# Attention, router and experts on one core: the first expert's first two columns made together between the turns, a tighter account for the search, and a last scatter of half rows

## The chip, the cores and the metric

One core of one Trainium2 chip runs the whole program. The metric is the time of one execution on the device in microseconds (us); lower is better. Times of a run vary: three runs of the kernel before took 895.05, 895.93 and 897.81 us.

## The reference

Two stages, cut to what matters. Attention over 8 x 12 heads of 448 tokens and 64 dimensions, with RMS norms on q and k, gives x of 3584 tokens by 768. A mixture of experts then assigns each token to one of 8 experts, greedily from the largest logit down, at most 448 tokens per expert, and sends it through that expert alone:

```python
logits = x @ w_gate
order = np.argsort(-logits.flatten())
for idx in order:
    tok, e = idx // E, idx % E
    if assigned[tok] >= 0 or counts[e] >= cap:
        continue
    assigned[tok] = e; counts[e] += 1
for e in range(E):
    h = np.maximum(x[assigned == e] @ w1[e], 0.0)
    out[assigned == e] = h @ w2[e]
```

## The kernel before, in words

The first 400 us are the attention, which the change does not touch. It leaves in DRAM `xd`, a row per token with two float16 halves (high and low part) of its 768 values, and the logits in SBUF.

**Router.** The greedy assignment is done expert by expert: the expert that is full first is found, its 448 tokens are listed, they and the expert are taken out, and the search starts again. `Router.phase(k)` (L1508) makes the steps of the k-th search. The first (k = 0) runs by itself between attention and experts. Searches 1 to 7 run as *hops* beside the experts' matmuls. A search of k = 1 to 6 has `open_bests` (VectorE finds each token's best open expert), then eight digits of four bits; each digit is `count` (four short TensorE matmuls, L1471, then VectorE's `own` and `cs`), `total` (one matmul, L1485, then VectorE's `ged`, L1488) and `accumulate` (one matmul, L1492, then VectorE's `v` and the comparison `cmp`, L1455). After the last digit come `place`, `slots`, the listing, `lists` (L1643) and `joined` (L1657), which leaves `idx`, 448 token numbers as 128 partitions by 4 columns; the fourth column uses 64 partitions.

**Experts.** Class `Experts`, L1700 on. The weights of the k-th expert come in eight pieces of 768 KB (`fetch`, L1736, issued by SyncE into four `stage` buffers; pieces 0 to 3 are w1, two columns each, 4 to 7 are w2). `split` (L1753) has ScalarE write the high float16 part and VectorE, in two halves, the low part (L1766). The second half's end frees the buffer for the piece four later. `gather` (L1772) brings the expert's rows by four indirect DMAs of GpSimd, chunks of 128, 128, 128 and 64 tokens. They have to be turned: by a transposing DMA, or, for experts 0 and 1, by TensorE (`turn_here`, L1788): per chunk twelve transposes into two PSUM tiles, one of the high half (i = 0) and one of the low (i = 1), each then copied into `xt` by ScalarE (L1801) or VectorE (L1803).

`hidden(k, f)` (L1817) makes column f of eight: 128 hidden values for all 448 tokens, 18 matmuls (L1848: six blocks, high by high, high by low, low by high), then ScalarE's relu into `hh` and VectorE's rest `hl`. For the first column of the first expert it has four parts of 128, 128, 128 and 64 tokens, with the turns of chunks 1, 2 and 3 between them; chunk 0 is turned ahead of it, in `run`. `result(k, c)` (L1851) makes 128 tokens' output in two halves of 384 columns (L1865), or for the last 64 tokens both halves at once on two halves of the array (L1874), copies them out scaled, and scatters the rows by an indirect DMA of GpSimd (L1884). In the last expert's last rows ScalarE copies one half and VectorE the other (L1880).

**The order of the work.** Every engine executes its instructions in the order in which the program issues them, so where the program puts a hop decides who waits. An account does this. `tick` (L1892) adds the estimated length of each matmul to a time `t`. Three lists hang on it: `fills` (a piece's `split`, at a given `t`), `lows` (VectorE's subtractions and the next fetch, not before an estimated time `low[0]`, 4 us later while the search has hops left, since `WAIT` = 4.0), and the `queue` of hops. A hop goes when `t >= due`. Ahead of a hop with TensorE work the oldest ready entry of `lows` is issued (L1904 on):

```python
if pe:
    for low in [low for low in self.lows if low[0] <= self.t + pe][:1]:
        self.low(low)
f()
self.t += pe
if dve:
    self.free = max(self.free + pre, self.t + self.REACH) + dve
    self.due = self.free + self.SLACK[len(self.router.e) > 1]
```

`free` is the account's guess of when VectorE is through, `SLACK` (L1917) what is added before TensorE may ask for the result: 0.3 us in search 1 and 0.45 us later. The copies of `turn_here` are not in `free`.

**Between router and first expert**, in `run` (L1980 on): the first search, the first two fetches, warm matmuls of 512 columns whose result nobody reads (`warm`, numbers in `WARM`), the gather, two more fetches that wait for the third chunk of rows, `open_bests` with the first comparison of search 1, four warm matmuls, `split` of piece 0, its two subtractions with the first `count` between them, three warm matmuls, the turn of chunk 0, the first `total`, and `t` is set to 0. From there the loop over experts runs, with `fills` for pieces 1 to 7 at 4.2 i - 2.3.

## Time and profile before

| | before |
|---|---|
| median of three runs (lowest, highest) | 895.93 us (895.05, 897.81) |
| the profiled execution: its time | 895.94 us |
| its span, first to last instruction | 894.0 us |
| mean granted TensorE clock (share of full speed) | 0.986 |
| TensorE busy | 857.7 us, 96% of the span |
| VectorE, ScalarE, GpSimd busy | 639.5, 470.1 and 384.4 us |
| first turns of the first expert | at 424.36 us |
| last matmul begins | at 884.86 us |

A row of a timeline has the start in us from the span's start, the length in us, the engine (PE is TensorE, PEld its weight load, DVE VectorE, ACT ScalarE, POOL GpSimd, SP SyncE; a q behind it is the engine's queue of instructions), the line of the kernel, the operation, what it writes and reads, and how many instructions are merged in the row. In square brackets stands the idle time before it and what ended that. Ends of matmuls are modelled: in a stream, the distance from start to start is what one costs. A row of a stage by windows has the stretch, its length, and for each engine the busy time and the number of instructions, then the granted clock (1.00 is 2.4 GHz, 0.50 is 1.2 GHz), the share of the DMA engines and GB/s.

### The profile page before, as it was taken

What the parts mean: (1) busy time and instruction counts of PE and PEld (TensorE: products, weight loads), DVE (VectorE), ACT (ScalarE), POOL (GpSimd) and SP (SyncE); (2) the same over time, 40 slices, a digit from 0 to 9 for tenths busy, and PEclk for the clock granted to TensorE, in tenths of its full rate; (3) what the DMA queues carried; (4) which work ended last, traced back from release to release, by engine and by line L of the source; (5) the groups of instructions that cost most, each with busy time, mean ns of one, the idle gap of its engine ahead of it and who ended that gap; (6) DMA issues with size and microseconds to landing.
All of it is one profiled execution on the core that took longest, in us unless ns stands there. A gap on an engine that the chain in (4) does not pass through costs nothing.

```text
span 894.0 us, 27400 instructions
## 1 busy us (share of the span) xinstructions
PE 857.7 (96%) x11671; PEld 554.2 (62%) x11673; DVE 639.5 (72%) x1573; ACT 470.1 (53%) x752; POOL 384.4 (43%) x390
## 2 busy tenths in 40 slices
PE   6999999999999999986999999999999999999996
PEld 2567676777777777874656565565555655555553
DVE  8999999989988986658877776776768567253100
ACT  6987887888778777550534333332434323343110
POOL 8899998889889887001012030110211021200001
PEclk9999999999999999996999999999999999999999
DMA  7679998999999987424647095693928659690001
GB/s 190 165 169 202 185 198 176 205 192 208 194 208 214 171 190 176 76 95 137 237 140 259 10 290 179 203 256 106 295 78 261 181 174 271 215 239 39 27 18 45
DMA packets 253011, 153.61 MB, mean 172 GB/s; under 512 B 178650, under 2 KB 240090, under 8 KB 251866
## 3 DMA queue, kind: packets, MB, share of 16 engines
q1 hardware_dynamic: 247832, 129.62, 60.4%
q0 software_dynamic: 4640, 22.02, 7.5%
q8 instruction: 91, 1.49, 0.7%
q14 instruction: 30, 0.25, 0.1%
q10 hardware_dynamic: 418, 0.23, 0.1%
HBM read 94.42 MB, written 22.02 MB: 130 GB/s over the span
## 4 chain that ended last, share of the span: by engine, by line
PE 56%; issue 22%; DVE 8%; DMA 4%; POOL 4%; ACT 3%; SPq 2%; POOLq 0%; ACTq 0%; DVEq 0%
PE ph L1848 13%; PE po L609 12%; PE psc L574 11%; PE py L1865 11%; DVE mx L555 3%; PE py L1874 2%; PE pm L544 2%; DMA q<-qs 2%; POOL out_dram L1884 2%; POOL rows L1781 1%; ACT e L585 1%; PE psc L544 1%; DMA q<-mt 1%; DMA stage<-in_moe_w_dram 1%; SPq L255 1%
## 5 line engine op out<-in xcount | busy, mean ns | idle before, releaser
L1848 PE MATMUL ph<-xt,w1h 128*128 128x448 f16 (+2 forms) x804 | 210.0, 344 | 0.1
L609 PEld LDWEIGHTS po<-v,e 128*64 128x64 f32 (+1 forms) x5376 | 172.2, 137 | 40.0 <-issue 20.4
L609 PE MATMUL po<-v,e 128*64 128x65 f32 (+1 forms) x5376 | 185.9, 223 | 1.6 <-DVE xt L376 1.0
L585 ACT ACTIVATE e<-psc 128x896 f32<-128x896 f32 x168 | 151.1, 915 | 47.1 <-PE psc L574 41.0
L574 PE MATMUL psc<-q,k 128*64 128x448 f16 x1344 | 155.9, 354 | 2.5 <-issue 1.3
L1884 POOL DMA_INDIRECT out_dram<-y,idx x32 | 33.4, 1042 | 285.3 <-ACT y L1867 250.3
L1848 PE MATMUL ph<-xt,w1l 128*128 128x448 f16 (+2 forms) x402 | 135.0, 344 | 0.0
L1865 PE MATMUL py<-w2h,hh 128*128 128x384 f16 x384 | 125.0, 326 | 0.0
L1865 PE MATMUL py<-w2l,hh 128*128 128x384 f16 x384 | 125.0, 326 | 0.0
L1865 PE MATMUL py<-w2h,hl 128*128 128x384 f16 x384 | 125.0, 326 | 0.0
L1848 PEld LDWEIGHTS <-w1h 128*128 128x128 f16 x804 | 73.9, 97 | 62.3 <-issue 1.9
L555 DVE TENSOR_REDUCE mx<-pm 128x2 f32<-128x896 f32 x96 | 104.0, 1084 | 10.6 <-PE pm L544 8.0
L1836 ACT ACTIVATE hh<-ph 128x448 f16<-128x448 f32 x64 | 34.8, 543 | 140.7 <-PE ph L1848 131.3
L1865 PEld LDWEIGHTS <-hh 128*128 128x128 f16 x768 | 73.5, 97 | 46.6
L574 PEld LDWEIGHTS <-k 128*64 128x64 f16 x1344 | 74.3, 110 | 32.4 <-issue 7.3
L1867 ACT ACTIVATE y<-py 128x384 f32<-128x384 f32 x48 | 23.5, 490 | 126.2 <-PE py L1865 100.4
L1781 POOL DMA_INDIRECT rows<-xd,idx x32 | 31.7, 991 | 125.8 <-DMA stage<-in_moe_w_dram 40.8
L555 DVE TENSOR_REDUCE mx<-psc 128x2 f32<-128x896 f32 (+1 forms) x74 | 77.8, 1056 | 3.2 <-PE psc L544 2.6
L1766 DVE SCALAR_TENSOR_TENSOR w2l<-stage,w2h 128x768 f16<-128x768 f32 x64 | 60.2, 952 | 24.3 <-ACT w2h L1762 24.3
L1838 DVE SCALAR_TENSOR_TENSOR hl<-ph,hh 128x448 f16<-128x448 f32 x64 | 39.4, 619 | 49.8 <-ACT hh L1836 49.6
L1766 DVE SCALAR_TENSOR_TENSOR w1l<-stage,w1h 128x768 f16<-128x768 f32 x64 | 59.3, 951 | 3.7 <-ACT w1h L1762 3.7
L1848 PEld LDWEIGHTS <-w1l 128*128 128x128 f16 x402 | 38.2, 97 | 30.9 <-issue 0.5
(300 smaller groups left out, 1438.9 us busy)
## 6 DMA issues: line engine op xcount, KB each, us to landing
stage<-in_moe_w_dram SPq DMA_DIRECT2D x64, 768.0 KB
vraw<-in_v_dram SPq DMA_DIRECT2D x24, 384.0 KB
xd<-xb SPq DMA_DIRECT2D x8, 1152.0 KB
qkraw<-in_q_dram SPq DMA_DIRECT2D x23, 384.0 KB
qkraw<-in_k_dram SPq DMA_DIRECT2D x23, 384.0 KB
vraw<-in_v_dram SPq DMA_DIRECT2D x24, 64.0 KB
xd<-xm SPq DMA_DIRECT2D x16, 96.0 KB
qkraw<-in_k_dram SPq DMA_DIRECT2D x22, 64.0 KB
```

The costliest lines, as they stand in the source:

```text
L544: nc.tensor.matmul(p[:, i, :448], qt[:, 128 * u:128 * u + 128], kt[:, 448 * s:448 * s + 448], start=True, stop=True)
L555: self.nc.vector.tensor_reduce(m, p[:, :k, :448], axis=AX.X, op=OP.max)
L574: nc.tensor.matmul(p[64 * h:64 * h + 64, i, :448], kt[:, a, n + 64 * h:n + 64 * h + 64], qt[:, a, 448 * s:448 * s + 448], start=st, stop=n ...
L585: self.nc.scalar.activation(e, p[:, :, :448], AF.Exp, scale=scale)
L609: self.nc.tensor.matmul(self.po(pair)[64 * n:64 * n + 64, w], self.T["e", d][r, i, q:q + 64], self.v1[g % 2][r, self.slot(a, u, s)], start ...
L1766: self.later(0.93, lambda w=w: self.nc.vector.scalar_tensor_tensor(l[:, w], v[:, w], self.WS, h[:, w], op0=OP.mult, op1=OP.subtract), k, i)
L1781: nc.gpsimd.indirect_dma_start(out=g[:n, c, :], out_offset=None, in_=self.xd, in_offset=bass.IndirectOffsetOnAxis(ap=idx[:n, c:c + 1], axi ...
L1836: nc.scalar.activation(hh, whole, AF.Relu)
L1838: self.later(0.6, lambda: nc.vector.scalar_tensor_tensor(hl, whole, 0.0, hh, op0=OP.max, op1=OP.subtract), k, 3.5, f)
L1848: nc.tensor.matmul(p, a[:, i, c], x[:, b, o], start=j == 0, stop=j == 17)
L1865: nc.tensor.matmul(p, a[:, f, s], b[:, f, o], start=st, stop=sp)
L1884: st = nc.gpsimd.indirect_dma_start(out=self.out, out_offset=bass.IndirectOffsetOnAxis(ap=self.router.idx[k][:n, c:c + 1], axis=0), in_=y[ ...
```

## The change

Four things are done.

- The start (`columns`, new, called at the first expert's begin). Columns 0 and 1 are made in three strips of 128, 128 and 192 tokens, in the order: turns of chunks 0 and 1, strip 0 of columns 0 and 1, turn 2, strip 1 of column 0, turn 3, strip 1 of column 1, strip 2 of both. For k = 0, ScalarE copies each chunk's high half and VectorE its low half. Within a strip the six matmuls with `w1l` come last. Pieces 0 and 1 are both split by ScalarE ahead of it, and piece 0's subtractions are issued there; piece 1's and the next two fetches go into `lows` for 2.5. `t` is 0 ahead of the first turn, and the first hop falls due at 2.5 (`SECOND`).
- `open_bests` of search 1 is a hop of its own, issued by hand; the first digit with its comparison is the next, left to the account. One warm matmul of four and the later three are gone.
- `SLACK` goes from 0.3 and 0.45 to 0.1 and 0.15.
- The last 64 tokens of the last expert: ScalarE copies both halves in one instruction, 128 partitions of 384 columns, and the scatter writes 128 half rows, with a list of half rows (`halves`) that search 7 makes out of `idx` with a few VectorE instructions (`both`, `half`, `halves`).

```diff
--- before.py
+++ after.py
@@ -1651,6 +1651,8 @@
                 f()
             both = st["both"] = self.small("both", [128, 2, 8, 2], BF)
             V.tensor_copy(both.rearrange("p i a t -> p (i a t)"), p)
+            if last:
+                V.tensor_copy(both[:, :, 7], q[:, :, 6])
             if k == 0:
                 st["gone"]()
 
@@ -1672,6 +1674,12 @@
             V.tensor_copy(lo, q[:, 1])
             idx = self.idx[k] = self.w.tile([128, 4], I32, name="idx", bufs=8)
             V.tensor_tensor(idx, q[:, 0], lo, op=OP.add)
+            if last:
+                half = self.small("half", [128, 1])
+                V.memset(half, 0.0)
+                V.memset(half[64:], 1.0)
+                self.halves = self.small("halves", [128, 1], I32)
+                V.scalar_tensor_tensor(self.halves, idx[:, 3:4], 2.0, half, op0=OP.mult, op1=OP.add)
 
         def many(*fs):
             return lambda: [f() for f in fs]
@@ -1689,7 +1697,11 @@
         else:
             begin, count, total, accumulate = self.digit_search(st)
             n = len(self.DIGITS)
-            hops.append((many(self.open_bests, lambda: self.digit(0), begin), 0.0, best + 1.0, 0.0))
+            if k == 1:
+                hops.append((self.open_bests, 0.0, best, 0.0))
+                hops.append((many(lambda: self.digit(0), begin), 0.0, 1.0, 0.0))
+            else:
+                hops.append((many(self.open_bests, lambda: self.digit(0), begin), 0.0, best + 1.0, 0.0))
             for i in range(n):
                 hops.append((lambda i=i: count(i), 0.12, counted, 0.0 if i else 1.05))
                 hops.append((lambda i=i: total(i), 0.12, 0.25, 0.0))
@@ -1797,12 +1809,12 @@
                                     idn[:n, :n])
             self.t += 0.34
             o = self.T["xt", k][:, 6 * i:6 * i + 6, 128 * c:128 * c + n]
-            if i and (k or c < 2) or k + c == 0:
+            if bool(i) == (k > 0):
                 nc.scalar.activation(o, p, AF.Copy)
             else:
                 nc.vector.tensor_copy(o, p)
 
-    WARM = 6, 4, 5, 4, 3
+    WARM = 6, 4, 5, 3
 
     def warm(self, n, after=None):
 
@@ -1819,34 +1831,41 @@
         if f == 0:
             T["hh", k] = self.w.tile([128, 8, 448], F16, name="hh", bufs=1)
             T["hl", k] = self.w.tile([128, 8, 448], F16, name="hl", bufs=1)
-        x = T["xt", k]
-        whole = self.ps.tile([128, 512], F32, name="ph", bufs=3)[:, :448]
-        c = slice(128 * f, 128 * f + 128)
-        parts = 4 if k + f == 0 else 1
         if k and f == 0 and k not in self.early:
             for n in self.HERE.get(k, ()):
                 self.turn_here(k, n)
-        for q in range(parts):
-            o = slice(448 * q, 448) if parts == 1 else slice(128 * q, min(448, 128 * q + 128))
-            if parts > 1:
-                for n in ((1,), (), (2, 3), ())[q]:
-                    self.turn_here(k, n)
-            self.column(k, whole[:, o], x, c, o, parts)
+        whole = self.begun.pop(f) if k == 0 and f in self.begun else self.column(k, f)
         hh, hl = T["hh", k][:, f], T["hl", k][:, f]
         nc.scalar.activation(hh, whole, AF.Relu)
         self.scalar(0.55)
         self.later(0.6, lambda: nc.vector.scalar_tensor_tensor(hl, whole, 0.0, hh, op0=OP.max, op1=OP.subtract), k, 3.5, f)
 
-    def column(self, k, p, x, c, o, parts):
+    def column(self, k, f, o=slice(0, 448), p=None):
+
         nc, T = self.nc, self.T
-        h, l = T["w1h", k], T["w1l", k]
-        each = [((h, i, i), (h, i, 6 + i), (l, i, i)) for i in range(6)]
-        order = [w for e in each for w in e]
-        if parts > 1:
-            order = [w for e in each for w in e[:2]] + [e[2] for e in each]
+        h, l, x = T["w1h", k], T["w1l", k], T["xt", k]
+        if p is None:
+            p = self.ps.tile([128, 512], F32, name="ph", bufs=3)[:, :448]
+        c, n = slice(128 * f, 128 * f + 128), o.stop - o.start
+        order = [w for i in range(6) for w in ((h, i, i), (h, i, 6 + i), (l, i, i))]
+        if n < 448:
+            order.sort(key=lambda w: w[0] is l)
         for j, (a, i, b) in enumerate(order):
-            nc.tensor.matmul(p, a[:, i, c], x[:, b, o], start=j == 0, stop=j == 17)
-            self.tick(0.189 if parts == 1 else 0.05)
+            nc.tensor.matmul(p[:, o], a[:, i, c], x[:, b, o], start=j + o.start == 0, stop=j == 17 and o.stop == 448)
+            self.tick(0.189 if n == 448 else max(0.057, n / 2400 + 0.003))
+        return p
+
+    SECOND = 2.5
+
+    def columns(self):
+
+        q = slice(0, 128), slice(128, 256), slice(256, 448)
+        for what in (0, 1, (0, 0), (1, 0), 2, (0, 1), 3, (1, 1), (0, 2), (1, 2)):
+            if isinstance(what, int):
+                self.turn_here(0, what)
+            else:
+                f, n = what
+                self.begun[f] = self.column(0, f, q[n], self.begun.get(f))
 
     def result(self, k, c):
         nc, T = self.nc, self.T
@@ -1874,16 +1893,18 @@
                         nc.tensor.matmul(p[64 * half:64 * half + 64], a[:, f, s],
                                          b[:, f, 384 * half:384 * half + 384], start=st, stop=sp)
                     self.tick(0.183)
-            for half in range(2):
-                o, i = y[:64, 384 * half:384 * half + 384], p[64 * half:64 * half + 64]
-                if k == 7 and half:
-                    nc.vector.tensor_scalar(o, i, sc, None, op0=OP.mult)
-                else:
+            if k == 7:
+                nc.scalar.activation(y[:, :384], p, AF.Copy, scale=sc)
+            else:
+                for half in range(2):
+                    o, i = y[:64, 384 * half:384 * half + 384], p[64 * half:64 * half + 64]
                     nc.scalar.activation(o, i, AF.Copy, scale=sc)
         nc.gpsimd.memset(self.spacer, 0.0)
-        st = nc.gpsimd.indirect_dma_start(
-            out=self.out, out_offset=bass.IndirectOffsetOnAxis(ap=self.router.idx[k][:n, c:c + 1], axis=0),
-            in_=y[:n], in_offset=None)
+        if k == 7 and n < 128:
+            to, at, y = self.out.rearrange("n (h d) -> (n h) d", h=2), self.router.halves, y[:, :384]
+        else:
+            to, at, y = self.out, self.router.idx[k][:n, c:c + 1], y[:n]
+        st = nc.gpsimd.indirect_dma_start(out=to, out_offset=bass.IndirectOffsetOnAxis(ap=at, axis=0), in_=y, in_offset=None)
         for o in self.scat:
             self.tc.declare_no_dep(st.ins, o.ins, reason="every token is in one list once")
         self.scat.append(st)
@@ -1914,7 +1935,7 @@
             self.due = self.free + self.SLACK[len(self.router.e) > 1]
 
 
-    REACH, SLACK, WAIT = 0.25, (0.3, 0.45), 4.0
+    REACH, SLACK, WAIT = 0.25, (0.1, 0.15), 4.0
 
     def scalar(self, us):
 
@@ -1980,7 +2001,7 @@
     def run(self):
         self.t = self.due = self.free = self.act = 0.0
         self.lows = []
-        self.now, self.waiting, self.early = 0, [], set()
+        self.now, self.waiting, self.early, self.begun = 0, [], set(), {}
         first, slots, rest = self.router.phase(0)
         first()
         self.load(0)
@@ -1998,16 +2019,14 @@
         hops = phases[0][0]
         hops.pop(0)[0]()
         self.warm(self.WARM[3], self.router.score[:, 0, 0:8])
-        self.step(0, 0)
-        first, second = self.lows[:2]
-        self.low(first)
-        hops.pop(0)[0]()
-        self.low(second)
-        self.warm(self.WARM[4])
-        self.turn_here(0, 0)
-        hops.pop(0)[0]()
-        self.t = self.due = self.free = 0.0
-        for i in range(1, 8):
+        for i in range(2):
+            self.step(0, i)
+        for low in self.lows[:2]:
+            self.low(low)
+        self.lows = [(self.SECOND, *low[1:]) for low in self.lows]
+        self.t = self.free = self.act = 0.0
+        self.due = self.SECOND
+        for i in range(2, 8):
             self.fill(self.FIRST * i - 2.3, 0, i)
         for k in range(1, 8):
             hops, ends, listing, lists, joined = phases[k - 1]
@@ -2022,6 +2041,8 @@
         for k in range(8):
             self.now = k
             self.start()
+            if k == 0:
+                self.columns()
             for f in range(8):
                 self.need(k, f // 2)
                 for low in [low for low in self.lows if low[3][1:] == (3.5, f - 2)]:
```

## Rows read from the trace of the kernel before

**Rows 1.** Page, costliest groups: line, engine, out<-in, count | busy us, mean ns | idle before.

```profile
L1848 PE MATMUL ph<-xt,w1h 128*128 128x448 f16 (+2 forms) x804 | 210.0, 344 | 0.1
```

**Rows 2.** Timeline of PE, from the first turns to the third column.

```profile
424.36 0.83 PE L1796 MATMUL py<-ident,rows 128*128 128x128 f16 x12
...
425.60 0.17 PE L1485 MATMUL rp<-cs,sums 128*128 128x8 f16 x1 [0.41 <-DVE cs L1481]
...
426.77 0.77 PE L1848 MATMUL ph<-xt,w1h 128*128 128x128 f16 x11
...
428.73 1.48 PE L1796 MATMUL py<-ident,rows 128*128 128x128 f16 x24
...
432.23 0.17 PE L1485 MATMUL rp<-cs,sums 128*128 128x8 f16 x1 [0.37 <-DVE cs L1481]
...
432.37 0.54 PE L1848 MATMUL ph<-xt,w1h 128*128 128x448 f16 x2
...
435.94 0.54 PE L1848 MATMUL ph<-xt,w1h 128*128 128x448 f16 x2
```

**Rows 3.** Timeline of ACT, the first split and the first turn's copies.

```profile
420.34 1.48 ACT L1762 ACTIVATE w1h<-stage 128x1536 f16<-128x1536 f32 x1 [4.20 <-DMA stage<-in_moe_w_dram]
425.21 1.51 ACT L1801 ACTIVATE xt<-py 128x768 f16<-128x768 f16 x2 [3.38 <-PE py L1796]
```

**Rows 4.** Timeline of PEld, the weight loads of the second turn.

```profile
425.60 0.68 PEld L1796 LDWEIGHTS <-rows 128*128 128x128 f16 x12 [0.53 <-DMA rows<-xd,idx]
```

**Rows 5.** Timeline of DVE in the same stretch.

```profile
424.38 0.67 DVE L1289 TENSOR_SCALAR digi<-keyi 128x28 int32<-128x28 int32 x7
...
429.26 1.55 DVE L1803 COPY xt<-py 128x768 f16<-128x768 f16 x4 [1.72 <-PE py L1796]
430.73 0.95 DVE L1766 SCALAR_TENSOR_TENSOR w1l<-stage,w1h 128x768 f16<-128x768 f32 x1
```

**Rows 6.** PE by timeline and by windows, where the granted clock fell and rose.

```profile
391.61 0.84 PE L720 MATMUL psc<-ident,xb 128*128 128x128 f16 x12
...
398.00:398.50 0.50, 0.50 (x32) 0.50 (x26) 0.00 (x0) 0.00 (x0) 0.00 (x0) 0.72 1.08 428
...
415.84 1.91 PE L1814 MATMUL py<-rows,ones 128*128 128x512 bf16 x4 [0.22 <-issue]
...
418.00:419.00 1.00, 0.70 (x19) 0.62 (x20) 0.74 (x6) 0.00 (x0) 0.00 (x0) 0.65 1.07 357
...
421.91 1.02 PE L1814 MATMUL py<-rows,ones 128*128 128x512 bf16 x4
```

**Rows 7.** Timelines of DVE and PE, a comparison and its count in a later search.

```profile
592.19 0.39 DVE L1455 TENSOR_TENSOR cmp<-v,rows 128x448 bf16<-128x448 bf16 x1
...
593.00 0.27 PE L1471 MATMUL rp<-oh,cmp 128*128 128x64 bf16 x4
```

**Rows 8.** Timeline of PE behind the second expert's turns.

```profile
485.41 0.33 PE L1874 MATMUL py<-w2l,hh 128*64 128x384 f16 x2
485.89 0.17 PE L1485 MATMUL rp<-cs,sums 128*128 128x8 f16 x1
```

**Rows 9.** Timelines of ACT, DVE, POOL at the end; landing of L1884; the end's drains.

```profile
881.21 0.49 ACT L1867 ACTIVATE y<-py 128x384 f32<-128x384 f32 x1 [3.36 <-PE py L1865]
885.28 0.48 ACT L1882 ACTIVATE y<-py 64x384 f32<-64x384 f32 x1 [3.58 <-PE py L1874]
...
885.80 0.56 DVE L1880 TENSOR_SCALAR y<-py 64x384 f32<-64x384 f32 x1 [26.79 <-ACT y L1882]
...
881.97 0.97 POOL L1884 DMA_INDIRECT out_dram<-y,idx  x1 [6.74 <-ACT y L1867]
...
886.63 0.90 POOL L1884 DMA_INDIRECT out_dram<-y,idx  x1 [3.60 <-DVE y L1880]
...
DMA to landing us min/median/max: 3.0/3.7/5.9
...
L2080 POOLq DRAIN  x1: 6525/6525/6525, 886.4 to 886.4; - x1
```

## The prediction, before the change was run

> **What bounds the kernel now.** I read the list of costliest groups first. It names TensorE: the largest group, 804 of the experts' matmuls, has 0.1 us of idle time ahead of all of them together [rows 1], so from the first expert's second column on, work saved on another engine is worth nothing, and only three things can move the time: when that full stretch begins, waits that the change puts into it, and what follows its last matmul. I then read TensorE's timeline around the beginning. The first expert's turns begin at 424.36, its second column at 432.37 and its third at 435.94 [rows 2]. A 128-column matmul takes (0.77 - 0.22) / 10 = 0.055 us there, so a strip of 18 takes 1.0; the second column, 18 matmuls of 448 columns, takes 3.57 with three search steps in it, 0.19 each; two chunks' turns take 1.48, 0.7 a chunk [rows 2]. A strip of 192 columns lies between: 0.055 + (0.19 - 0.055) x 64 / 320 = 0.082, 1.5 a strip. Work of TensorE from 424.36 to 435.94 is four turns (2.8), the first column (3.5) and the second (3.4), with seven steps some 10.0 of 11.6 us. The rest is waiting: 0.41 and 0.37 us for `cs` of the search [rows 2], some 0.5 us at 426.3 while ScalarE copies both halves of the first chunk, 0.75 us each [rows 3].
>
> **The change, the start.** Going are the three last warm matmuls, the first digit's begin, count and total ahead of and between the turns, and the two-copies-on-one-engine order. Coming is a written order: turns 0 and 1, strips (column 0, chunk 0) and (1, 0), turn 2, (0, 1), turn 3, (1, 1), then both 192-wide strips. TensorE's work is the same: two columns of 1.0 + 1.0 + 1.5 = 3.5 against 3.5 + 3.4. What can be won is waiting.
>
> Turn 0 may go some tenths earlier without the warm matmuls, but that is worth nothing, since turn 1 loads its weights only at 425.60, after 0.53 us put down to the gathered rows [rows 4]. From there: turn 1 to 426.3; two strips to 428.3 (ScalarE and VectorE copy the halves side by side, 0.75 and about 0.5 us [rows 3, 5], so no wait at 426.3; the second piece's split is in front of ScalarE's copy, but ScalarE stands idle from 421.8, where the first split ends, to 425.21, and a split is 1.48 us [rows 3]); turn 2 to 429.0; strip to 430.0; turn 3 to 430.7; strip to 431.7; two wide strips to 434.7; five search steps, 0.3: 435.0. That is 0.9 us earlier than 435.94 if nothing waits.
>
> Something will wait. In the account, turns are 0.68 and a strip 1.03, so begin falls due at 2.5, inside the second strip, count at the first matmul after turn 2, total at the first after turn 3, and accumulate at 6.7, twelve matmuls into that strip, at about 431.5 on the chip. VectorE by then has: its copy of turn 2 (0.5, from 429.2), seven digits (0.67), `own` and `cs` to about 430.8, its copy of turn 3 (0.35), then, because a hop takes the oldest waiting subtraction ahead of itself, one `w1l` half (0.9 net) and only then `ged` [durations: rows 5]: 432.3. Accumulate waits 0.8 us. The same order, copies, a `w1l` half, then the step, is what makes the 0.37 us wait at 432.23 now [rows 2, 5]. The account knows nothing of the copies, and the change takes 0.2 us of its slack. Bounds are 0 (the subtraction falls behind `ged`) and 0.9; I take 0.5, since the order was worked by hand and one place's shift removes it. So the third column starts at 435.5, and three steps that were done by 435.94 are still to come, 0.15: **start -0.3 us**, bounds -0.9 and +0.4.
>
> The clock speaks against the new start. Between the warm matmuls at 421.91 and the first strip TensorE will have little but two turns, since three warm matmuls and a count are gone. The row: from 391.61 on it had transposes and then gate matmuls of 8 or 16 columns, and the clock left 1.00 only in the half microsecond from 398.0 (0.72), over 6 us later [rows 6]. A stretch of 3.7 us (422.6 to 426.3) with two turns in it is milder, so I cost it at nothing. The Trainium skill ("TensorE: Matmul & The Clock Gate", Part 4: PE-mode transpose) says that transposes do not count as TensorE being busy for the clock; in this trace the clock held through transposes and narrow matmuls for 6 us, which gives the rule no support, but does not refute it either. By that rule the result would be the second rival.
>
> **The change, the slack.** The search is nowhere late: TensorE does not wait for its result. Begin moves some 4 us later, and 0.2 us less slack on each of some 24 steps gives the first search that back, so the second expert's loads keep their time; for later searches 0.3 us a step only ends them sooner. No gain. The cost is bounded by two places. The smallest step margin in a later search that I found is 0.42 us (`cmp` ends 592.58, the count goes at 593.00 [rows 7]); less 0.3 leaves 0.12, no wait. At the second expert's turns, where VectorE's copies again are not in the account, TensorE goes from 485.41 to 485.89 where 0.16 is the normal gap [rows 8], 0.3 us lost, and 0.3 less slack can double it. **Slack +0.2 us**, bounds 0 and +0.8.
>
> **The change, the tail.** Now ScalarE copies one half to 885.76, VectorE the other to 886.36, and GpSimd starts the scatter at 886.63 [rows 9]. One copy of 128 partitions is as long as one of 64 (0.49 and 0.48 us [rows 9]); the scatter starts 0.6 earlier, at 886.03. It has 128 half rows instead of 64 rows: 0.97 against 0.90 us on GpSimd [rows 9]. Its landing (3.0 to 5.9, median 3.7 us [rows 9]) is not what ends the run; GpSimd's drain of 6.53 us from 886.4, to 892.9 [rows 9], is, and I know nothing of how it depends on the rows. If on nothing: 0.6 - 0.07 = 0.5. If it grows as the landing does from its least to its median, 0.7 is lost again. **Tail -0.5 us**, bounds -0.6 and +0.2: the drain starts as the scatter is issued, and moves with it. The VectorE operations for the half-row list, one cast, two memsets, one multiply-add, fall in the last search, with the experts' stretch of TensorE over them; without that cover, under 1 us.
>
> **Sum.** -0.3 + 0.2 - 0.5 = -0.6 us. The profiled execution took 895.94 us (span 894.00 and 1.94 around it), 0.01 from the median of the three runs, so 895.94 - 0.6 = 895.3.
>
> **Rivals.** (a) *The waits really go*: accumulate finds `ged` done, start -0.9, slack 0, tail -0.5: 894.5. For: the turns' copies are shared better. Against: VectorE's queue above. (b) *The clock falls in the new gap* after 422.6. Price: 512-column warm matmuls take 0.43 us before and 0.21 us after it rises [(1.91 - 0.61) / 3 and (1.02 - 0.38) / 3, rows 6], so work goes at half speed; it rose within the microsecond from 418.0 (0.65 there), after warm matmuls from 415.84 on [rows 6], some 2.9 us, and as long a stretch of strips at half speed loses half of it, 1.5: 895.3 + 1.5 = 896.8. Against: rows 6 as read above. (c) *The slack was needed*: slower. It decides at the counts and totals of the six later searches' 144 steps, from the point where VectorE is more than 0.12 us later than its account; one step in six waiting 0.2 us is 24 x 0.2 = 4.8: 900.1. For: 0.42 is the margin of an undisturbed step, and a step with a `w2l` half in front has less to spare. Against: the account already holds such halves at 0.93. (d) *The tail gives nothing*, the drain growing with the rows: 895.3 + 0.5 = 895.8.
>
> **How the numbers follow.** A measurement here tells 0.3%, 2.7 us, from no change: 893.2 and 898.6 are the limits. Forecast 0.60, (a) 0.15, (b) 0.10, (c) 0.08, (d) 0.07. Only the lower end of (a), with all three terms at their best and the scatter of the runs (895.05 to 897.81), passes 893.2: 0.08. Slower is (c): 0.08. Within: 0.84. The range goes from the sum of the low bounds, -0.9 + 0 - 0.6 = -1.5, 894.4, less 0.7 for scatter, to the sum of the high ones, +1.4, 897.3, which takes (b) in: 893.7 to 897.3.
>
> **What would show it.** Right: no TensorE wait at 426.3, third column near 435.5, one wait of about half a microsecond on `ged` in the strip after turn 3; granted clock 1.00 from 419 on; last matmul some 0.1 us earlier than now; one copy of about 0.49 us, then the scatter 0.27 us later, and a drain of about 6.5 us. Wrong: a granted clock of 0.50 after 422; waits of TensorE at many counts and totals past 490; a drain near 7 us; a second expert that waits for weights or rows because the first search ended late.

## The result, and the profile after

The changed kernel takes 902.7 us (899.22 to 905.09, 6 runs) against 895.5 (894.38 to 897.81, 6 runs) beside it: ratio 1.0082, 95% interval 1.0068 to 1.0097, **slower by 7.2 us**, outside my range. The profiled execution took 905.09 us, the most of the six; its span is 903.2, its mean granted clock 0.979.

The page, its group of experts' matmuls and its row of clock slices:

```profile
PE 861.6 (95%) x11687; PEld 558.4 (62%) x11687; DVE 636.1 (70%) x1575; ACT 471.1 (52%) x753; POOL 385.1 (43%) x390
PEclk9999999999999999977999999999899999999999
L1854 PE MATMUL ph<-xt,w1h 128*128 128x448 f16 (+2 forms) x816 | 211.5, 345 | 0.0
```

The group that I read first [rows 1] has even less idle time ahead of it than before, though the kernel is 7 us slower. Idle time is booked to the group whose instruction ends it, and here that is a search step's short matmul between two of these. The waits of TensorE from 500 to 700 us show it (line, what it waited for, us in total, times, longest); the same question of before gets an empty answer:

```profile
PE rp L1471 <- DVE cmp L1455: 4.0, 1, 4.0
PE rp L1485 <- DVE cs L1481: 3.9, 2, 3.2
```

To place the loss I measure from a row that both kernels have in common, the last listing step of the first search. It comes 2.85 us earlier in the profiled execution of after, with the same code ahead of it, so that is scatter between executions. From that row to the end of the span after's profiled execution takes 12 us more than before's, where the medians differ by 7.2: the sizes below are those of a long execution. PE timelines, after and then before:

```profile
412.09 0.20 PE L1572 MATMUL rp<-xs,ones 128*128 128x56 bf16 x1 [1.51 <-DVE xs L1540]
```

```profile
414.94 0.21 PE L1572 MATMUL rp<-xs,ones 128*128 128x56 bf16 x1 [1.51 <-DVE xs L1540]
```

The stretches between first columns of experts, from TensorE's timelines (the last kernel is the third experiment below):

| us | before | after | after, gather behind loads |
|---|---|---|---|
| that row | 414.9 | 412.1 | 413.4 |
| from it to the second expert | 74.3 | 75.4 | 74.2 |
| second and third expert | 115.0 | 116.6 | 115.8 |
| fourth expert | 57.7 | **63.4** | 57.1 |
| fifth expert | 57.6 | **63.0** | 57.2 |
| sixth to last matmul | 165.3 | 164.0 | 164.0 |
| start of the last matmul to the end | 9.14 | 8.67 | 8.62 |
| span | 894.0 | 903.2 | 890.3 |

The loss is for the most part in two experts, 5.7 and 5.4 us. Here is the first of the two places: timelines of POOL, SP, ACT, DVE and PE of after, in the order of the chain (L1793 gathers, L1798 is a turning DMA, L1762 a fetch, L1774 and L1778 the split, L1481 to L1485 a total):

```profile
609.89 1.46 POOL L1793 DMA_INDIRECT rows<-xd,idx  x1 [3.06 <-DVE idx L1676]
614.28 10.88 SPq L1798 DMA_TRANSPOSE xt<-rows  x3
626.11 3.94 SPq L1762 DMA_DIRECT2D stage<-in_moe_w_dram  x4
631.27 1.48 ACT L1774 ACTIVATE w1h<-stage 128x1536 f16<-128x1536 f32 x1 [5.24 <-DMA stage<-in_moe_w_dram]
632.79 0.96 DVE L1778 SCALAR_TENSOR_TENSOR w1l<-stage,w1h 128x768 f16<-128x768 f32 x1 [3.40 <-ACT w1h L1774]
634.02 0.23 DVE L1481 TENSOR_REDUCE cs<-own 128x8 f16<-128x72 f16 x1
630.71 0.35 PE L1854 MATMUL ph<-xt,w1h 128*128 128x448 f16 x1
634.30 0.17 PE L1485 MATMUL rp<-cs,sums 128*128 128x8 f16 x1 [3.24 <-DVE cs L1481]
```

Read it from below. TensorE starts nothing between 630.71 and 634.30, because the total wants `cs`. VectorE made `cs` late, since in its queue a subtraction of the fifth expert's first piece stood ahead and waited 3.40 us for ScalarE's split; that had waited 5.24 us for the weights. The weights were fetched late, at 626.11 (214.0 us after the common row, 10.9 later than before, 618.09 below), because SyncE's queue had three turning DMAs of the same expert ahead of the fetches. Those took 10.88 us, and the first of them had waited for the gathered rows before, with the fetches behind it. SyncE's waits from 600 to 700 us, in after:

```profile
SPq L1798 <- DMA rows<-xd,idx: 45.3, 2, 23.5
```

Two waits, the longer 23.5 us, one at each of the two places; before has such waits too (20.5 us in two), but with the first four loads ahead of them. The second place is alike (SP, ACT and PE of after):

```profile
674.51 7.62 SPq L1798 DMA_TRANSPOSE xt<-rows  x2
683.03 3.23 SPq L1762 DMA_DIRECT2D stage<-in_moe_w_dram  x4
687.91 1.48 ACT L1774 ACTIVATE w1h<-stage 128x1536 f16<-128x1536 f32 x1 [5.45 <-DMA stage<-in_moe_w_dram]
691.02 0.28 PE L1471 MATMUL rp<-oh,cmp 128*128 128x64 bf16 x4 [4.03 <-DVE cmp L1455]
```

Before, the loads of that fifth expert stood 13 us ahead of its first turning DMA, and its gather came 8 us behind them (SP and POOL of before):

```profile
618.09 2.98 SPq L1750 DMA_DIRECT2D stage<-in_moe_w_dram  x4
631.36 2.33 SPq L1786 DMA_TRANSPOSE xt<-rows  x1
626.53 0.99 POOL L1781 DMA_INDIRECT rows<-xd,idx  x1 [19.98 <-DVE idx L1674]
```

Why the order turned: with the tighter margins the searches end earlier. The gathers of the third, fourth and fifth expert, counted from the common row, begin at 107.4, 158.9 and 211.6 us before and at 104.9, 148.8 and 197.8 after: 2.5, 10.1 and 13.8 us sooner. The program issues `feed(k)`, an expert's first four fetches, only when the expert before has no piece left to split; `gather(k)` and the turning DMAs that follow it by the account have no such condition. So the turning DMAs overtake the loads in the order of the program: one, three and two of them for the fourth, fifth and sixth expert, none before.

In this execution both idle stretches cost again through the clock. Windows of after at the first; the third number from the end is the granted clock:

```profile
630.00:632.00 2.00, 1.06 (x6) 0.44 (x5) 0.00 (x0) 0.72 (x1) 0.00 (x0) 1.00 1.02 339
632.00:634.00 2.00, 0.00 (x0) 0.00 (x0) 1.19 (x3) 1.70 (x3) 0.00 (x0) 0.84 1.08 367
634.00:636.00 2.00, 1.70 (x6) 0.74 (x6) 1.18 (x4) 0.97 (x1) 0.00 (x0) 0.50 1.10 351
638.00:640.00 2.00, 2.00 (x11) 1.03 (x10) 1.69 (x6) 1.46 (x2) 0.00 (x0) 0.50 1.02 381
640.00:642.00 2.00, 2.00 (x14) 1.22 (x13) 0.55 (x4) 0.00 (x0) 0.00 (x0) 0.95 0.00 0
```

TensorE runs at 1.2 GHz from 634 to about 640. TensorE's wait itself is 3.24 us, the expert lost 5.7: the rest is mostly this (the fourth experiment has a wait of nearly this length without it).

**The start** has, in this execution, my rival (b). PE timeline and windows of after:

```profile
421.22 1.04 PE L1808 MATMUL py<-ident,rows 128*128 128x128 f16 x12 [1.39 <-DMA rows<-xd,idx]
423.83 1.46 PE L1854 MATMUL ph<-xt,w1h 128*128 128x128 f16 x12
430.45 0.16 PE L1492 MATMUL rp<-flagd,times8.0_8247 128*128 128x1 bf16 x1 [0.62 <-DVE ged L1488]
433.92 0.54 PE L1854 MATMUL ph<-xt,w1h 128*128 128x448 f16 x2
```

```profile
420.00:421.00 1.00, 0.00 (x0) 0.00 (x0) 1.00 (x2) 1.00 (x1) 0.70 (x2) 1.00 0.81 270
422.00:423.00 1.00, 0.69 (x8) 0.43 (x6) 0.56 (x1) 0.58 (x1) 0.00 (x0) 0.50 0.90 330
424.00:425.00 1.00, 1.00 (x12) 1.00 (x10) 0.86 (x4) 0.24 (x1) 0.37 (x3) 0.50 0.06 12
```

The clock falls after an idle microsecond (420 to 421) and stays at 0.50 for some 3.5. The third column comes 21.83 us after the common row, against 21.00 before [rows 2].

**The tail** (ACT and POOL timelines, and the drain's line, shortest, middle and longest in ns):

```profile
894.95 0.49 ACT L1897 ACTIVATE y<-py 128x384 f32<-128x384 f32 x1 [3.58 <-PE py L1893]
895.72 0.97 POOL L1907 DMA_INDIRECT out_dram<-y,halves  x1 [3.02 <-ACT y L1897]
L2101 POOLq DRAIN  x3: 46/109/6592, 895.5 to 902.9; - x3
```

One copy of 0.49 us, a scatter 0.28 us behind it, a drain of 6.59 us against 6.53 [rows 9]: 8.67 us from the last matmul's start to the end, 0.47 less than before.

### The profile page after: what moved, and what is told of

The parts are those of the page before. It is cut to its first block, busy times and chain, and to the rows that moved or that the text cites. A ratio compares the mean times of both kernels' runs of the same rounds, so it can differ in the third digit from the quotient of the medians.

```text
span 903.2 us, 27429 instructions
## 1 busy us (share of the span) xinstructions
PE 861.6 (95%) x11687; PEld 558.4 (62%) x11687; DVE 636.1 (70%) x1575; ACT 471.1 (52%) x753; POOL 385.1 (43%) x390
## 5 line engine op out<-in xcount | busy, mean ns | idle before, releaser
L1884 PE MATMUL py<-w2h,hh 128*128 128x384 f16 x384 | 125.6, 327 | 0.0
L1884 PE MATMUL py<-w2l,hh 128*128 128x384 f16 x384 | 125.6, 327 | 0.0
L1884 PE MATMUL py<-w2h,hl 128*128 128x384 f16 x384 | 125.4, 327 | 0.0
L555 DVE TENSOR_REDUCE mx<-pm 128x2 f32<-128x896 f32 x96 | 104.1, 1084 | 10.1 <-PE pm L544 7.5
L1884 PEld LDWEIGHTS <-hh 128*128 128x128 f16 x768 | 73.4, 98 | 45.9 <-issue 1.1
L1778 DVE SCALAR_TENSOR_TENSOR w2l<-stage,w2h 128x768 f16<-128x768 f32 x64 | 60.0, 951 | 23.8 <-ACT w2h L1774 23.8
L1778 DVE SCALAR_TENSOR_TENSOR w1l<-stage,w1h 128x768 f16<-128x768 f32 x64 | 60.1, 952 | 14.8 <-ACT w1h L1774 14.7
L1793 POOL DMA_INDIRECT rows<-xd,idx x32 | 32.6, 1019 | 69.5 <-PE ph L1854 27.2
```

The lines of the kernel that those rows point to most:

```text
L555: self.nc.vector.tensor_reduce(m, p[:, :k, :448], axis=AX.X, op=OP.max)
L1778: self.later(0.93, lambda w=w: self.nc.vector.scalar_tensor_tensor(l[:, w], v[:, w], self.WS, h[:, w], op0=OP.mult, op1=OP.subtract), k, i)
L1793: nc.gpsimd.indirect_dma_start(out=g[:n, c, :], out_offset=None, in_=self.xd, in_offset=bass.IndirectOffsetOnAxis(ap=idx[:n, c:c + 1], axi ...
L1884: nc.tensor.matmul(p, a[:, f, s], b[:, f, o], start=st, stop=sp)
```

## Experiments

Times stand beside runs of the kernel before on the same chip: 894.8 us for the first four, 894.7 for the next four, 895.1 for the last three. The first and the fourth expectation count experts from 0, the text counts from 1.

**The margins alone**, in the kernel before:

```diff
-    REACH, SLACK, WAIT = 0.25, (0.3, 0.45), 4.0
+    REACH, SLACK, WAIT = 0.25, (0.1, 0.15), 4.0
```

> The kernel before with the slack of 0.1 and 0.15 us alone. In the program's order for SyncE, one turning DMA of the third expert's rows (counted from 0) now stands ahead of that expert's weight loads, and two of the fourth's; before and with the wide slack none does. Order theory (the weights come late behind the turning DMAs, a subtraction waiting for them blocks VectorE, and the search step behind it blocks TensorE): one wait of 2 to 5 us of TensorE at a search step near 630, with the clock at 0.50 after it, little or nothing near 690, and a time of 898 to 902. Margin theory (VectorE is simply too late at many steps): waits of 0.1 to 0.4 us at many steps all through the searches, none above 1 us, and 898 to 905. Start theory (the loss comes from the new start): no change, 895.5.

897.8 us, ratio 1.0049 (1.0021 to 1.0077). One turning DMA stands ahead of the fourth expert's loads, two ahead of the fifth's; TensorE waits 0.97 us until 573.2 and 0.80 until 626.2, far less than the 2 to 5 us that I expected, and the granted clock stays at 1.00 behind both. The margins alone make it slower, by less than the whole change.

**The whole change with the old margins**:

```diff
-    REACH, SLACK, WAIT = 0.25, (0.1, 0.15), 4.0
+    REACH, SLACK, WAIT = 0.25, (0.3, 0.45), 4.0
```

> The changed kernel with the slack back at 0.3 and 0.45 us. SyncE's order is that of the kernel before again. Order and margin theory both: the two waits near 630 and 690 are gone, 895 to 896.5, with the start some 0.8 us longer than before (granted clock 0.50 around the first turns) and the end 0.5 us shorter. Start theory: still 900 or more.

899.5 us, ratio 1.0058 (1.0031 to 1.0084): not the 895 to 896.5 that I expected, and the ten runs lie far apart (892.89 to 903.9; the profiled one took 902.52). In it the two waits are gone, and another is there. TensorE's wait, then the timelines of SP and POOL of this kernel:

```profile
PE ph L1854 <- DMA xt<-rows: 5.6, 1, 5.6
```

```profile
533.69 10.38 SPq L1798 DMA_TRANSPOSE xt<-rows  x2
526.03 0.98 POOL L1793 DMA_INDIRECT rows<-xd,idx  x1 [34.48 <-PE rp L1604]
```

The new start begins the search beside the experts some 5 us later (its first count goes 14.0 us after the common row, 8.6 before). With the old margins the gather of the third expert is 111.5 us after that row (107.4 before), and the third expert's rows are not turned when TensorE wants them. So the margins are boxed in: too wide, and rows are late; too tight, and loads are late.

**The whole change, the gather held behind the loads**, in `start`:

```diff
+            if w[0] == self.gather and (self.feed, w[1]) in self.waiting:
+                continue
```

> The changed kernel, slack 0.1 and 0.15 kept, but an expert's gather is held back until its weight loads have been issued, so no turning DMA stands ahead of them. Order theory: no wait of TensorE above 1 us, time as with the old slack, 895 to 896.5. Margin theory: as slow as the changed kernel, 900 or more, with its waits at the steps.

892.4 us, ratio 0.9979 (0.9964 to 0.9994): faster than both kernels, with the tight margins kept. Timelines of POOL, SP and ACT at the place of the first wait:

```profile
609.15 1.46 POOL L1793 DMA_INDIRECT rows<-xd,idx  x1 [3.06 <-DVE idx L1676]
602.33 17.03 SPq L1762 DMA_DIRECT2D stage<-in_moe_w_dram  x4
619.47 8.22 SPq L1798 DMA_TRANSPOSE xt<-rows  x3
625.19 1.48 ACT L1774 ACTIVATE w1h<-stage 128x1536 f16<-128x1536 f32 x1
```

The gather is as early as in after (609.89), the fetches now stand ahead of the turning DMAs, and the split at 625.19 waits for nothing. That settles it for the order on SyncE: the search's steps are as tight as in after, and no wait of TensorE over 0.8 us is left behind the common row.

**The first subtractions 6 us later** in the account, for the experts from the third on: the two halves that stood ahead of `cs` and `cmp` move back (in `split` and `later`; a length of 0.930001 us instead of 0.93 marks piece 0 of such an expert).

```diff
-        self.lows.append((self.act + self.REACH, us, f, of))
+        self.lows.append((self.act + self.REACH + (6.0 if us == 0.930001 else 0.0), us, f, of))
```

> The changed kernel with the turning DMAs still ahead of the weight loads (three and two of them, for the fourth and fifth expert), but each expert's first two low-part subtractions may go only 6 us later in the account, so that they do not stand ahead of a search step on VectorE while the weights are still coming. Order theory, if the wait passes through VectorE's queue as the trace has it: the weights are as late (ScalarE waits 4 to 6 us for them), but TensorE's waits near 630 and 690 fall below 1 us and the time to 895 to 897.5. If TensorE is held by the weights or by ScalarE's queue instead, the waits and 900 or more stay. Margin theory: 900 or more.

901.8 us, ratio 1.0095 (1.0066 to 1.0124). The wait only changes its road (ACT, DVE, PE; then a window):

```profile
633.40 1.48 ACT L1774 ACTIVATE w1h<-stage 128x1536 f16<-128x1536 f32 x1 [6.01 <-DMA stage<-in_moe_w_dram]
635.35 0.62 DVE L1841 SCALAR_TENSOR_TENSOR hl<-ph,hh 128x448 f16<-128x448 f32 x1 [3.55 <-ACT hh L1839]
636.11 0.16 PE L1492 MATMUL rp<-flagd,times8.0_8247 128*128 128x1 bf16 x1 [3.10 <-DVE ged L1488]
636.00:638.00 2.00, 1.89 (x15) 1.11 (x15) 0.69 (x4) 1.76 (x2) 0.00 (x0) 1.00 1.10 359
```

ScalarE's waiting split has the relu `hh` behind it, VectorE's `hl` waits for that, and `ged` stands behind `hl`. Late loads stop TensorE through either queue, as the expectation had it for the case that ScalarE's queue holds it. In this execution the clock stays at 1.00 behind the wait of 3.10 us, and the fourth expert takes 60.6 us, 2.9 more than before; in after it was a wait of 3.24 us, a clock of 0.50 behind it and 5.7 more. By this comparison the fall of the clock is worth some 2.5 us there, and it does not follow every such wait.

**The tail alone**: the kernel before with the diff's hunks of `phase` and `result`, among them

```diff
-            for half in range(2):
...
+            if k == 7:
+                nc.scalar.activation(y[:, :384], p, AF.Copy, scale=sc)
```

> The kernel before with the last rows' part alone: one ScalarE copy of 128 partitions, the list of half rows, one scatter of 128 half rows. If the tail is worth what the changed kernel's profile shows (last matmul to the end of the span 8.67 us against 9.14), 0.5 us are won: 894.3 to 895.4 us beside a before of 894.8 to 895.5, ratio 0.9994 or so, which five rounds hardly tell from 1; the profile tells: last matmul to end 8.6 to 8.7 us, the scatter about 0.3 us behind the copy, the drain 6.5 to 6.6 us. If the drain grows with the number of rows, the stretch stays at 9.1.

893.7 us, ratio 0.999 (0.9979 to 1.0001); last matmul to end 8.70 us. The eleven profiles with the new tail give 8.62 to 8.82 us there, the two with the old one 9.14 and 9.29. The profile shows the half microsecond; the time does not tell it from no change.

**Old start with the gate, the margins and the tail**: the kernel of the tail alone, with

```diff
-    REACH, SLACK, WAIT = 0.25, (0.3, 0.45), 4.0
+    REACH, SLACK, WAIT = 0.25, (0.1, 0.15), 4.0
...
+            if w[0] == self.gather and (self.feed, w[1]) in self.waiting:
+                continue
```

> The gated kernel with the start of before: slack 0.1 and 0.15, gather behind the weight loads, new tail, old start. It prices the start on a ground without the long waits. By the changed kernel's profile the new start is 0.8 us slower up to the third column (its clock falls): then this one takes 891.6 us, 0.8 less than the 892.4 of the gated kernel. By the prediction's working (start -0.3 us) it takes 892.7. If the gated kernel's gain over before (some 2.5 us) came from the start, it is at 894 to 895.

894.3 us, ratio 0.9996 (0.9986 to 1.0006), 1.9 us more than the gated kernel's first result and 0.6 more than its second (below). By its number this is my last case (894 to 895, the gain comes from the start). But the three results are from three chips; by their ratios the new start is 1.1 to 1.5 us better, the common row alone scatters by 3.3 us, and by the second expert's first column the starts can't be told apart (see below). What the start is worth in the median stays open, other than that it does not cost 0.8 us.

**Eleven warm matmuls ahead of the first turn**, with the gate:

```diff
-    WARM = 6, 4, 5, 3
+    WARM = 6, 4, 5, 4, 7
...
             self.low(low)
+        self.warm(self.WARM[4])
```

> The kernel with the gather behind its weight loads (892.38 us), and ahead of the first turn four and seven warm matmuls instead of three. Theory: in the new start the granted clock falls to 0.50 because TensorE has nothing to do between the last warm matmul and the first turn; with the warm matmuls it stays at 1.00 from 420 to 427, and the third column comes some 1 to 1.5 us earlier counted from the end of the attention, the time about 1 us lower, 891.3 us. Rival: the first turn waits longer behind the added matmuls (seven are 1.5 us) than the clock costs, so 892 to 893. Rival: the clock falls anyway, because the turns themselves don't hold it: then the slots 422 to 425 show 0.50 again.

895.3 us, ratio 1.0008 (0.9995 to 1.0021): no gain over before, and the gated kernel's is lost. Windows of its profiled execution (892.29 us, the second shortest of eleven):

```profile
422.00:423.00 1.00, 0.40 (x8) 0.23 (x5) 0.56 (x1) 0.81 (x1) 0.00 (x0) 1.00 0.75 299
424.00:425.00 1.00, 1.00 (x22) 1.00 (x19) 0.85 (x4) 0.56 (x1) 0.00 (x0) 1.00 0.07 25
```

Like after, this execution comes to 420 us at clock 1.00, and with the gap filled it does not fall. But the third column is at 21.76: turn 1 waits 0.80 us for gathered rows, and a total 0.53 for `cs` behind a subtraction. In the seven other profiles with the new start the clock was still at 0.50 up to 421 to 424 and rose about as the turns began. So whether the fall hits depends on the execution, and one execution of each kind shows no more than that the filled gap can hold the clock.

**Search 1 alone tight** (the first beside the experts), in the changed kernel:

```diff
-    REACH, SLACK, WAIT = 0.25, (0.1, 0.15), 4.0
+    REACH, SLACK, WAIT = 0.25, (0.1, 0.45), 4.0
```

> The changed kernel with SLACK (0.1, 0.45): only the first search beside the experts (the one that starts late) is tight, the six later ones have the margin of before. SyncE then has every expert's first four weight loads ahead of its turning DMAs, without the gate. If the two limits are the whole story (second search late: third expert's rows late; later searches early: turning DMAs ahead of the loads), both are gone: no TensorE wait over 1 us at 546, 577, 631 or 687, and the time is that of the gated kernel or up to 3 us more, 892 to 895.5 us. If tight steps themselves cost (many small waits) there is nothing to see here either, but the gated kernel already speaks against that. If rows are still late for the third expert: 2 to 5 us at 546, 897 to 900 us.

904.6 us, ratio 1.0113 (1.0097 to 1.0129): a miss. The gather of the third expert is 112.0 us after the common row, no sooner than with both old margins, and TensorE waits 5.0 us for turned rows. The search for the second expert ends 55.8 us after that row, against 57.0 with the old margins: 0.2 us on 24 steps gave 1.2 us and not 4.8. Why was not tried. The search after it takes 55.3 us from list to list here and 48.0 in after: there 0.3 us a step gave its 7.2. So search 2 is the one that must be tight.

**Searches 1 and 2 tight, the later ones as before**:

```diff
-            self.due = self.free + self.SLACK[len(self.router.e) > 1]
+            self.due = self.free + self.SLACK[len(self.router.e) > 2]
```

with `SLACK` (0.1, 0.45).

> The changed kernel with the tight margin (0.1 us) for searches 1 and 2 alone and that of before (0.45 us) for searches 3 to 7. In the run with the first search alone tight the second search still ended 112 us after the attention's last step, as with the old margins (111.5), against 105 in the changed kernel: there the third expert's turning DMAs came too late. Theory of two limits: the second search must end early enough for the third expert's rows, the later ones not ahead of the weight loads. Here SyncE has four weight loads ahead of every expert's turning DMAs, and the second search should end about 105 us after the attention: no TensorE wait over 1 us at 546, 577, 631 or 687, time 892 to 895 us. Rival (the margin of the later searches matters in itself, by their steps): 896 us or more, with many small waits, or none of the long ones gone.

895.3 us, ratio 0.9997 (0.9985 to 1.0009). The gather of the third expert comes 102.5 us after the common row, all first loads stand ahead of the turning DMAs without the gate, and no wait over 0.8 us is left: both limits are kept, and the 7 us are gone. The theory of two limits holds, though the time is that of before and not the gated kernel's.

**The gated kernel again**, and **with the second piece's subtractions later**:

```diff
-        self.lows = [(self.SECOND, *low[1:]) for low in self.lows]
+        self.lows = [(self.SECOND + 4.5, *low[1:]) for low in self.lows]
```

> The changed kernel with the gather held until its expert's weight loads are issued, once more, beside its variant and on a chip of its own draw: 892.4 us there against 894.8 before, ratio 0.9979. If that holds, 0.996 to 0.9995 again. The kernel with the old start, gate, slack and tail gave 0.9996, the tail alone 0.999; if the gain were luck of the first chip, the ratio here is 0.999 to 1.0.

> The gated kernel with the second piece's two subtractions (and the fetches behind them) due 4.5 us later in the account, so that the first accumulate's ged stands ahead of them in VectorE's queue. The prediction's step said that accumulate waits because one such half stands ahead of ged. If so, TensorE's 0.62 us wait at about 430.5 goes, and the third column comes 0.5 to 0.7 us earlier counted from the attention's end (20.6 in the gated kernel, so 20.0); the time 0.5 us under the gated kernel's. Rival: the wait moves to the next total, where the halves now stand, and the third column stays at 20.6; or column 2 waits for its low weights.

Again: 893.7 us, ratio 0.9984 (0.9973 to 0.9996). The gain over before is there a second time, 1.4 to 2.4 us by the medians. From the second expert's first column to the last matmul both profiles of the gated kernel take 394.1 us, the old start with the gate 394.8, before and the tail alone 395.6: so 1.5 us of the gain lie there and 0.5 in the tail. What makes the 1.5 was not looked for.

Variant: 894.0 us, ratio 0.999 (0.9978 to 1.0002). DVE and PE of the variant:

```profile
429.41 0.17 DVE L1488 TENSOR_SCALAR_CACHE_REDUCE ged<-rp 128x8 bf16<-128x8 f32 x1
433.38 0.54 PE L1854 MATMUL ph<-xt,w1h 128*128 128x448 f16 x2
```

`ged` is made right behind the copies, TensorE's wait for it is gone, and the third column is 19.8 us after the common row against 20.6. The fifth expert then has two waits, 0.42 and 0.76 us, near 668 that the gated kernel has not, and takes 1.5 us more. The time shows no gain.

## Why the prediction was wrong

**The step that failed** is "The search is nowhere late", "for later searches 0.3 us a step only ends them sooner. No gain", and with it the term **slack +0.2 us**, bounds 0 and +0.8. Alone the tight margins cost 3.0 us by the medians (1.9 to 6.9 by the ratio's interval); in after's profile the two late loads are about 11 of the 12.5 us that it loses from the common row to its last matmul (5.7 and 5.4 in two experts). I costed the steps, and there I was right: the gated kernel has the same steps and no such wait. I did not cost what a search that ends sooner *issues*: a gather, and on SyncE's queue four turning DMAs that wait for its rows, with the next weights behind them. Before's trace had the numbers. Loads 13.3 us ahead of the first turning DMA (618.09 to 631.36), and by my own estimate a gain of 24 x 0.3 = 7.2 us in each later search, one after the other: two searches' gain is more than that lead. The other half of the sentence, that 0.2 us less on 24 steps gives the first search its later begin back, failed too: it gave 1.2 us of some 5. And "No gain" was a little low: with the loads held ahead, tight margins under the old start take 0.8 us less from the second expert on (394.8 against 395.6).

**Rival (c)** had the sign and the part, not the mechanism. It looked for many waits of 0.2 us at steps that VectorE makes late; there are two waits of 3 to 4 us, and in this execution a lower clock behind each. My list of signs had "a second expert that waits for weights or rows because the first search ended late". Weights were late because searches ended early, and, with the old margins, rows because one ended late, each for a later expert than I named.

**Start, -0.3 us** (bounds -0.9 and +0.4): the third column is at 20.5 to 20.7 in the six executions of this start whose clock was up by then, against 21.0 before (20.8 to 21.2 in the four with the old start), so -0.3 to -0.5 beside before, as worked out. The wait for `ged` is 0.62 us where I took 0.5, and its cause, a `w1l` half ahead of it, is shown by the variant. **Rival (b)** came true in the profiled execution of after: 21.83, 1.2 us more than those six, where I had priced it at 1.5. I had set it at nothing because the clock held for 6 us through transposes and narrow matmuls [rows 6]. The same rows show it falling then, to 0.72 in a half microsecond in which TensorE was busy throughout (0.50 of 0.50 us); I should have read that as a warning. The Trainium skill ("TensorE: Matmul & The Clock Gate", Part 4: PE-mode transpose) says that transposes don't count as busy in the same way; here two turns followed an idle 1.39 us and the clock was down under them, which agrees with it, but the idle time alone could have done it: with the gap filled, the same turns ran at 1.00. By the second expert's first column the two starts can no longer be told apart: 74.2 to 74.8 us in those six, 73.9 to 74.9 in the four with the old start.

**Tail, -0.5 us**: 8.67 against 9.14, -0.47. The drain did not grow as the landing does: 0.07 us for twice the rows. Rival (d) falls.

**The range** left (c) out at 0.08. Its price, 4.8 us, was of the right order; its chance was not, because I asked only whether steps had slack to spare and not what the account's margins hold apart.

## What to carry to other kernels

Work that ends earlier issues its followers earlier, and on a queue that executes in order they can overtake something that is needed sooner: before tightening a schedule, list for each queue what stands within the time that is won. Where two kinds of transfer share a queue, write the order down as a condition (here two lines) and leave the timing free. And take "no idle time ahead of this group" only together with the waits of the short instructions between its members.

## What was not expected of the hardware

Turning DMAs hold SyncE's queue for a long time and unevenly: issuing one took 1.2 to 5.8 us of it in before and 1.2 to 7.1 in after (24 each), where a fetch of 768 KB took 0.4 in the median of both. And one whose rows have not landed holds what stands behind it as well, 23.5 us at the longest above. And the scatter of 128 half rows drains in 6.59 us, that of 64 whole rows in 6.53: twice the rows and the same bytes cost 0.07 us.
